# Row maxima of a sliding-window attention: one matmul of 384 columns for three key blocks, half a head group at a time

## Chip, core, metric

The kernel runs on one core of one Trainium2 chip, as one program. The metric is the device time of one execution in microseconds, the median of repeated runs. All computation is fp32; matrix products that need full accuracy are built from "fp32r" halves (a value is split into a high part and a remainder, and three of the four cross products are summed).

## What is computed

A mixer block over 2048 tokens of 512 channels. Attention has 32 heads of 16 channels and looks back over a window of 256 keys; its result is gated by an MLP on the same normalised input.

```python
S, D, H, Dh, W, F = 2048, 512, 32, 16, 256, 1792
xn = layernorm(x)
# attention
q, k, v = split(xn @ wqkv)                      # 32 heads of 16
scores = q @ k.T * Dh ** -0.5
mask = (i - j >= 0) & (i - j < 256)             # i: query, j: key
s = (softmax(where(mask, scores, -1e9)) @ v) @ wo
# gate
g = silu(gelu(layernorm(xn) @ w1 + b1) @ w2 + b2)
return x + s * g
```

## The kernel before, in words

**Stages.** Four layernorm chunks with the first projections (to about 60 us of the span), the attention (60 to 418 us), and the MLP with the output projection (418 us to the end).

**The attention's order is written out by hand.** The 32 heads are eight groups `n` of four heads; a group's four heads are two pairs `p`, and within a pair two heads `a`, one on rows 0 to 63 and one on rows 64 to 127 of the PE array, which run side by side (one such pair of matmuls is called a wave here). The loop over `u` makes 64 units: unit `u` takes key blocks `kb` and `kb + 1` of 128 keys of group `u // 8`. A unit is two steps, `t = 2u` and `t = 2u + 1`. Every call in the loop issues its instructions at once, and each engine runs them in the order in which they were issued (`Ordered` keeps that order for PE, DVE, ACT and POOL; SP, which issues the DMAs, has one queue too). `plan` (`at`) and `ends` (`behind`) hold what is to be issued in the middle and at the end of a given step; `fills` holds matmuls of other work that are laid into the steps: the q/k projections of later groups, the v projections (steps 56 to 73), and the MLP's first layer for the first 512 tokens (from step 98).

**A unit's work.** `prob_part(u, part)` multiplies keys with queries into the two banks of `stb` (8 waves a unit over three parts), ACT takes the exponential into `pt`, POOL zeroes what the mask forbids. `pv_part(u)` multiplies the probabilities with v into `otb`, columns of `zo`; ACT copies that to `oraw` (two buffers), and SP stores it to `oT_d` two steps on.

**The maxima.** The scores are shifted by each query's maximum before the exponential, by an extra row of the query operand. So the maxima of 128 queries (a block `qb`) are computed `LEAD` = 12 steps ahead: in step `t` those of block `m = t + 12`, one block a step. The window of a query block covers three key blocks: its own (lower triangle), the middle one (whole), and the one before that (upper triangle). `max_ends` multiplies with the two ends (one strided matmul of 256 columns for each of the four heads, into the two banks of `xy`); `copy_predicated` then overlays the two triangles with the mask `upper`, and a `tensor_reduce` takes the maximum. `max_middle` multiplies with the middle block (four matmuls of 128 columns into columns 0 to 255 of the two banks of `zo`, named `mids`), with a `tensor_reduce` of its own. `otb` lies in columns 256 to 511 of zo's second bank. Every fourth block `max_rows` takes the minimum of the (negated) two parts, splits it, transposes it and sends it through `mT_d` into the query operand.

**Order in a unit before.** Even step: `prob_part(u, 1)`, ends into xy, middle into zo; on DVE the copy, the reduction of zo, the reduction of xy; then fills. Odd step: `prob_part(u, 2)`, middle into zo with its reduction, two thirds of the fills, ends into xy with copy and reduction, `max_rows` if due, the rest of the fills, `prob_part(u + 1, 0)`, `pv_part(u)`. In the first unit of a group all fills of the odd step come after `prob_part(u + 1, 0)`.

**Other transfers.** `stage_in` copies `w1`, `w2` and `wo` into an order of its own in DRAM (16 steps of 4, from step 23). `keep_xt` stores the normalised input of chunks 1 to 3 (twelve transfers of 512 KB, every fourth step from 25 to 69). `fetch_scales` spreads a row of 512 per-token scales over 128 partitions; before, into a tile of its own at step 80 (`scales_0`) and again, after the attention, into `scales`.

**PSUM.** Eight banks of 512 fp32 columns: `xy`, `zo`, `stb` and `fb` have two each. The program orders any two engines that touch the same bank of one tile, whichever columns they touch.

Of the kernel before, what the change touches and what calls it, by code (L numbers as in the profile page):

```python
# [9 lines left out]
F32 = mybir.dt.float32  # L10
F32R = mybir.dt.float32r
I32 = mybir.dt.int32
# [37 lines left out]
def mixer_kernel(ctx, tc, x, wqk, wv, wo, w1, b1, w2, b2, out):  # L50
# [131 lines left out]
    zo = psum.tile([P, 2, 512], F32, name="zo")  # L182
    otb = zo[:, 1, 256:512]
    mids = zo[:, :, 0:256].rearrange("q a (p k) -> q a p k", p=2)
    ends_of = xy.rearrange("q a (p e k) -> q a p e k", p=2, e=2)
    psf = attn.enter_context(tc.tile_pool(name="psf", bufs=1, space=PSUM))
# [37 lines left out]
    clear_rows(0, ((nc.vector, 0, 1536), (nc.scalar, 4096, 7168), (nc.gpsimd, 1536, 4096), (nc.gpsimd, 7168, 8192)))  # L224
    scales = None
    mask = upper.bitcast(I32).unsqueeze(1).unsqueeze(1).to_broadcast([P, 2, 2, P])
    b1s = const.tile([P, NF], F32, name="b1s")
# [259 lines left out]
    def pair_h(f):  # L487

        def mm(ps, k, r, **flags):
            kt, (a, b) = k // 3, PASSES[k % 3]  # L490
            return nc.tensor.matmul(ps, w1_part(a, f)[r, P * kt: P * (kt + 1)], mlp["yy"][b][kt][r], **flags)

        def finish(ps, t, copy):
            raw = t2.tile([P, 512], F32, tag="t2", name=f"hr_{f}")
            if 5 < f < 12:
                copy(raw, ps)
            else:
                nc.vector.tensor_mul(raw, ps, scales)
            if f < 4:
                soon[f] = raw  # L500
            else:
                behind(t, nc.sync.dma_start, h_d[f - 6], raw)
        return 3 * KT, mm, finish
# [53 lines left out]

    def max_places(n, qb):

        if (n, qb // 4) not in mts:  # L560
            mts[n, qb // 4] = small.tile([P, 2, 2, 2, 4], F32, tag="mt", name=f"mt_{n}_{qb}", bufs=2)
        return (mts[n, qb // 4][:, i, :, :, qb % 4] for i in range(2))

    def max_ends(n, qb):

        mt, _ = max_places(n, qb)
        for p in range(2):
            for a in (1, 0):
                if qb < 2:
                    max_scores(ends_of[:, a, p, 0], n, qb, a, p, lambda row: row[:, P * qb: P * qb + 1].to_broadcast([64, P]))  # L570
                    max_scores(ends_of[:, a, p, 1], n, qb, a, p, lambda row: row[:, P * qb: P * (qb + 1)])
                else:
                    max_scores(ends_of[:, a, p], n, qb, a, p,
                               lambda row: row.rearrange("d (b k) -> d b k", k=P)[:, qb - 2: qb + 1: 2])
        own = ends_of[:, :, :, 1]
        outs["max"] = nc.vector.copy_predicated(own, mask, ends_of[:, :, :, 0]),
        return lambda: nc.vector.tensor_reduce(out=mt, in_=own, axis=AX.X, op=ALU.max, negate=True)

    def max_middle(n, qb):

        if qb == 0:
            return
        _, mu = max_places(n, qb)
        for p in range(2):
            for a in (1, 0):
                max_scores(mids[:, a, p], n, qb, a, p, lambda row: row[:, P * (qb - 1): P * qb])
        nc.vector.tensor_reduce(out=mu, in_=mids, axis=AX.X, op=ALU.max, negate=True)

    def max_block(n, qb):

        rest = max_ends(n, qb)
        max_middle(n, qb)
        rest()

    def max_rows(n, c, t):

        both = mts.pop((n, c))
        mt = both[:, 0]
        mh = small.tile([P, 2, 2, 2, 4], F32R, tag="mh", name=f"mh_{n}_{c}", bufs=2)
        pairs = slice(0 if c else 1, 4)  # L600
        nc.vector.tensor_tensor(mt[:, :, :, pairs], mt[:, :, :, pairs], both[:, 1, :, :, pairs], op=ALU.min)
        eng = nc.gpsimd if t >= -1 else nc.vector
        eng.tensor_copy(mh[:, :, 0], mt)
        eng.tensor_tensor(mh[:, :, 1], mt, mh[:, :, 0].bitcast(F32), op=ALU.subtract)
        mT = small.tile([P, 32], F32, tag="mT", name=f"mT_{n}_{c}", bufs=2)

        for fn, args in todo_dve:
            fn(*args)
        todo_dve.clear()
        nc.vector.transpose(mT, mh.rearrange("p a l i b -> p (a l i b)").bitcast(F32))  # L610
        rows = mT_d[n, c]

        def bring_in():
            nc.sync.dma_start(slots[n % 2][3:P:32, 0, :, 512 * c: 512 * (c + 1)].bitcast(F32),
                              rows.rearrange("(h p b) t -> h p (b t)", h=4, p=2))
        (at if t < 0 else behind)(t + (t < 0), nc.sync.dma_start, rows.rearrange("r (i t) -> i r t", i=4), mT)
        behind(t + 1 + (t < 0), bring_in)
# [46 lines left out]
    def pv_part(u):  # L664

        n, kb = u // 8, 2 * (u % 8)
        seq = [(kb, lambda j: pts[u, j // 2][:, j % 2, 128:384], 0, 256),
               (kb + 1, lambda j: pts[u, j // 2][:, j % 2, 0:128], 128, 256)]
        if kb:
            seq[:0] = [(kb - 1, lambda j: pts[u - 1, 2][:, j % 2, 256 * (j // 2): 256 * (j // 2 + 1)], 0, 256),  # L670
                       (kb - 2, lambda j: pts[u - 1, j // 2][:, j % 2, 384:512], 0, 128)]
        for i, (k, of, lo, hi) in enumerate(seq):
            for j in range(4):
                nc.tensor.matmul(otb[32 * j: 32 * j + DH + 1, lo: hi], vt[:, k, (4 * n + j) % 16], of(j),
                                 start=(i == 0), stop=(i == len(seq) - 1),
                                 skip_group_check=True, tile_position=(0, 32 * j))
        oraw = sgp.tile([P, 256], F32, tag="or", name=f"oraw_{u}", bufs=2)
        nc.scalar.copy(oraw, otb)
        cols = slice(P * kb, P * (kb + 2))
        at(2 * u + 2, nc.sync.dma_start, oT_d[n, :, :, cols].rearrange("j r t -> (j r) t"), oraw)  # L680
# [4 lines left out]
    def scale_parts():  # L685
# [20 lines left out]
        def power(c):  # L706
            at = sv[:, 4 * c: 4 * c + 4]
            nc.gpsimd.tensor_tensor(at, at, mhalf, op=ALU.pow)
        return variance, ratio, power

    def fetch_scales(c, dst):
# [165 lines left out]
    for b in range(4):  # L877
        behind(73 + b, nc.sync.dma_start, s_d[:, b], svT[32 * b: 32 * b + 4 * NCH])
    def open_scales():
        nonlocal scales  # L880
        scales = bigp.tile([P, 512], F32, tag="wa", name="scales_0")
        fetch_scales(0, scales)
    behind(80, open_scales)
    for k in range(KT * (NCH - 1)):
        behind(25 + 4 * k, keep_xt, 1 + k // KT, k % KT)
    by_vector = nc.vector.tensor_copy
# [8 lines left out]
    for f, t, lo_at, lo_by in ((6, 90, 93, nc.vector), (7, 95, 96, nc.vector), (8, 96, 98, on_pool), (9, 99, 101, nc.vector),  # L895
# [5 lines left out]
        at(lo_at, settle, "w1", f, None, lo_by)  # L901
    at(113, open_w2, 0)
    for f in range(W2_FIRST):
        at(114 + f // 2, fetch, "w2", f)
        at(121 + f, settle, "w2", f, by_vector, nc.vector)
# [10 lines left out]

    def first_h(f, scaled=True):

        for k in range(3 * KT):
            hidden_mm(fb[f], f, k)  # L920
        ready[f] = t2.tile([P, 512], F32, tag="t2", name=f"hf_{f}")
        if scaled:
            nc.vector.tensor_mul(ready[f], fb[f], scales)
        else:
            nc.vector.tensor_copy(ready[f], fb[f])

# [31 lines left out]

    def own_max(part, m):
        return part(m // 16, m % 16) if m < end else lambda: None  # L960

# [26 lines left out]
    for u in range(end // 2):  # L988
        t = 2 * u
        prob_part(u, 1)  # L990
        rest = own_max(max_ends, t + LEAD)
        own_max(max_middle, t + LEAD)
        rest()
        calm[0] = t < end - LEAD
# [5 lines left out]
        prob_part(u, 2)  # L1000
        own_max(max_middle, t + LEAD)
        todo = fills.get((t, 0), [])
        n = sum(fn.__name__ == "unit" for fn, _ in todo)
        now[:] = t, 0
        run(delayed.pop((t, 0), ()))
        n -= n if u % 8 == 0 else n // 3
        for fn, args in todo[:n]:
            fn(*args)
        planned(t)
        fill_in(t, 1)  # L1010
        own_max(max_ends, t + LEAD)()
        calm[0] = False
# [19 lines left out]
    nc.sync.on = False  # L1032
    first_h(1, False)

# [11 lines left out]
    scales = cp.tile([P, 512], F32, name="scales")  # L1046
    fetch_scales(0, scales)
    wos = cp.tile([P, 2, 4, 512], F32R, name="wos")
# [8 lines left out]

    nc.gpsimd.tensor_tensor(ready[1], ready[1], scales, op=ALU.mult)
    for f in range(6, NF, 2):
# [3 lines left out]
        for k in range(2 if f < 12 else 0):  # L1063
            nc.gpsimd.tensor_tensor(t[:, k], t[:, k], scales, op=ALU.mult)
        if f == 8:
            den = fetch_sums()
    nc.sync.dma_start(b2s, bass.AP(tensor=b2.tensor, offset=b2.offset, ap=[[0, P], [1, 512]]))

# [443 lines left out]
```

## Time and profile before

| what | value |
|---|---|
| median of 3 runs | 737.12 us (735.98 to 738.46) |
| the profiled execution | 737.41 us |
| its span, first to last instruction | 735.7 us |
| mean granted clock | 0.998 |
| busy: PE, DVE, ACT, POOL | 717.6, 507.7, 411.7, 298.9 us |

The profile shows one execution. Its views used here: the page (busy time by engine, groups of instructions with count, busy time and mean duration), the windows (busy time by stretch), the timeline (instructions in order of time, like ones merged: start, length, engine, operation, `out<-in`, count, idle time before and what ended it), the waits (who waited for whom: total us, times, longest) and the chain of waits (the work that ended last, followed back). "PEld" is the weight load ahead of a matmul. All instructions are recorded under the line of one helper (L42), so groups are told apart by their tiles: `xy<-qk` and `zo<-qk` are matmuls of the maxima, `zo<-pt,vt` the output (each fp32 matmul is recorded twice), `stb<-qk` the scores, `fb<-xnT,wqb` fills, `mt<-` the reductions.

### The profile page before, as it was taken

How to read it: one execution, taken by the hardware profiler on the slowest of the kernel's cores; microseconds unless marked ns; L12 is line 12 of the kernel's file. 1: busy time of each engine (PE TensorE's matmuls, PEld its weight loads, DVE VectorE, ACT ScalarE, POOL GpSimd, SP SyncE). 2: the span in 40 equal slices, each digit the busy share in tenths (PEclk: the TensorE clock that was granted, in tenths of full speed). 3: DMA queues.
4: the chain of work that ended last, by engine and by line, in shares of the span. 5: the costliest groups of instructions: out<-in, count | busy, mean ns of one | idle time of the engine just before them, and what ended most of it. 6: DMA issues, size and time to landing. Idle time of an engine off the chain costs nothing.

```text
span 735.7 us, 17763 instructions
## 1 busy us (share of the span) xinstructions
PE 717.6 (98%) x6944; PEld 580.7 (79%) x6944; DVE 507.7 (69%) x863; ACT 411.7 (56%) x628; POOL 298.9 (41%) x500
## 2 busy tenths in 40 slices
PE   8999999998899999999999999999999999999997
PEld 7998777776678887777777787888888888888886
DVE  7886787876677667778884667536687855667823
ACT  7767777766577566777877726232353734541001
POOL 7344666755468554676777550113202000001102
PEclk9999999999999999999999999999999999999999
DMA  8325455767787733667824465547213322163701
GB/s 294 79 48 126 96 137 142 201 179 205 200 236 202 207 113 97 160 157 192 222 75 153 154 219 147 195 130 238 91 58 104 104 79 86 63 186 113 253 16 58
DMA packets 66275, 106.95 MB, mean 145 GB/s; under 512 B 12624, under 2 KB 21072, under 8 KB 66192
## 3 DMA queue, kind: packets, MB, share of 16 engines
q1 hardware_dynamic: 66192, 105.82, 50.5%
q8 instruction: 55, 0.90, 0.5%
q14 instruction: 28, 0.23, 0.1%
HBM read 54.80 MB, written 33.82 MB: 120 GB/s over the span
## 4 chain that ended last, share of the span: by engine, by line
PE 90%; ACT 3%; DMA 3%; DVE 2%; issue 1%; SPq 0%; POOL 0%; ACTq 0%; DVEq 0%
PE acc L42 20%; PE fb L42 19%; PE zo L42 15%; PE p L42 9%; PE stb L42 7%; PE s L42 6%; PE h L42 6%; PE xy L42 5%; ACT pt L42 2%; PE pv L42 2%; DMA oT_d<-oraw 2%; DMA qk<-sh 1%; DVE mt L42 1%; DMA x<-in_x_dram 1%; SPq L42 0%
## 5 line engine op out<-in xcount | busy, mean ns | idle before, releaser
L42 ACT ACTIVATE pt<-stb 128x1024 f32<-128x1024 f32 (+1 forms) x176 | 177.7, 1009 | 51.7 <-PE stb L42 47.4
L42 POOL TENSOR_SCALAR_AFFINE_SELECT pt<-pt 128x512 f32<-128x512 f32 (+1 forms) x296 | 162.7, 569 | 86.7 <-ACT pt L42 85.8
L42 DVE COPY_PREDICATED xy<-upper,xy 128x512 f32<-128x512 int32 x128 | 88.9, 695 | 61.8 <-PE xy L42 61.6
L42 POOL TENSOR_TENSOR xo<-xo,gated 128x512 f32<-128x512 f32 x15 | 19.9, 1329 | 220.1 <-DVE gated L42 219.1
L42 PE MATMUL fb<-xnT,wqb 64*128 64x512 f32 (+2 forms) x732 | 105.9, 393 | 0.2 <-DVE xy L42 0.2
L42 PE MATMUL acc<-w,gh 128*128 128x512 f32 x320 | 98.7, 390 | 1.5 <-ACT gh L42 1.5
L42 PE MATMUL zo<-pt,vt 128*17 128x128 f32 (+1 forms) x1920 | 90.5, 327 | 0.0
L42 DVE TENSOR_REDUCE mt<-xy 128x4 f32<-128x512 f32 x128 | 88.0, 688 | 2.3
L42 DVE TENSOR_REDUCE mt<-zo 128x4 f32<-128x512 f32 x120 | 82.7, 689 | 6.9 <-PE zo L42 6.4
L42 PE MATMUL stb<-qk 64*128 64x384 f32 (+1 forms) x704 | 76.7, 296 | 2.1 <-ACT pt L42 2.1
L42 PEld LDWEIGHTS stb<-qk 64*128 64x128 f32 x704 | 58.9, 186 | 23.1 <-ACT pt L42 9.4
L42 PEld LDWEIGHTS zo<-pt,vt 128*17 128x17 f32 x1920 | 48.9, 97 | 33.3 <-issue 1.8
L42 PEld LDWEIGHTS acc<-w,gh 128*128 128x128 f32 x320 | 60.0, 188 | 14.3 <-ACT gh L42 1.9
L42 PEld LDWEIGHTS fb<-xnT,wqb 64*128 64x128 f32 (+1 forms) x732 | 61.8, 188 | 6.4 <-DVE xy L42 0.4
L42 PE MATMUL xy<-qk 64*128 64x256 f32 (+2 forms) x608 | 62.2, 291 | 1.1 <-DVE mt L42 1.1
L42 PE MATMUL acc<-w,gl 128*128 128x512 f32 x160 | 62.5, 391 | 0.0
L42 PEld LDWEIGHTS xy<-qk 64*128 64x128 f32 x608 | 48.6, 187 | 8.3 <-DVE mt L42 2.3
L42 PE MATMUL zo<-qk 64*128 64x128 f32 x480 | 48.8, 281 | 6.1 <-ACT oraw L42 5.4
L42 PE MATMUL p<-xnT 128*128 128x512 f32 x189 | 51.8, 389 | 0.0
L42 PEld LDWEIGHTS zo<-qk 64*128 64x128 f32 x480 | 36.3, 186 | 16.0 <-ACT oraw L42 6.9
L42 PE MATMUL s<-wos,ohl 128*128 128x512 f32 (+1 forms) x204 | 44.3, 377 | 0.0
L42 ACT ACTIVATE gated<-acc 128x512 f32<-128x512 f32 x16 | 8.7, 595 | 61.9 <-DVE acc L42 61.9
(210 smaller groups left out, 1212.4 us busy)
## 6 DMA issues: line engine op xcount, KB each, us to landing
qk<-sh SPq DMA_DIRECT2D x128, 128.0 KB
qk<-pjr SPq DMA_DIRECT2D x64, 128.0 KB
oT_d<-oraw SPq DMA_DIRECT2D x64, 128.0 KB
w_d<-in_w_dram SPq DMA_DIRECT2D x14, 512.0 KB
xt_d<-xnT SPq DMA_DIRECT2D x12, 512.0 KB
x<-in_x_dram SPq DMA_DIRECT2D x16, 256.0 KB
w<-w_d SPq DMA_DIRECT2D x16, 256.0 KB
or<-oT_d SPq DMA_DIRECT2D x16, 256.0 KB
```

Of the source, the lines that this page charges most:

```text
L42: r = issue(*args, **kwargs)
```

## The change

The maxima of one pair `p` (half of a block's four heads) become `max_part(n, qb, p)`: for each of the two heads one matmul of 384 columns over all three key blocks (blocks 0 and 1 of a group have fewer), pair 0 in the two banks of `xy`, pair 1 in the two banks of `zo`, columns 0 to 383. The function returns the DVE work: a `copy_predicated` of 256 elements that overlays the triangles, and one `tensor_reduce` of 512 over own and middle block. `max_rows` has no minimum to take any more. `otb` becomes columns 384 to 511 of both banks of zo, one bank for each of the unit's two query blocks; `pv_part` issues 24 matmuls of 128 columns instead of 16 of 256 and 128.

Order in a unit after: even step: pair 0's matmuls into xy, `prob_part(u, 1)`, pair 1's into zo, DVE's work for xy, then for zo, then fills. Odd step: `prob_part(u, 2)`, a quarter of the fills, pair 1 into zo with its DVE work, the other fills (in a group's first unit up to half of them), pair 0 into xy with its DVE work, `max_rows`, `prob_part(u + 1, 0)`, the remaining fills, `pv_part(u)`.

The first scales go into a free corner of w2's tile (`first_scales`), fetched at step 114; `first_h(1)` multiplies by them directly; the fetch into `scales` comes after that of the sums. `keep_xt` moves to every second step from 56 to 78.

```diff
-    otb = zo[:, 1, 256:512]
-    mids = zo[:, :, 0:256].rearrange("q a (p k) -> q a p k", p=2)
-    ends_of = xy.rearrange("q a (p e k) -> q a p e k", p=2, e=2)
+    otb = zo[:, :, 384:512]
...
-    scales = None
-    mask = upper.bitcast(I32).unsqueeze(1).unsqueeze(1).to_broadcast([P, 2, 2, P])
+    mask = upper.bitcast(I32).unsqueeze(1).to_broadcast([P, 2, P])
...
-                nc.vector.tensor_mul(raw, ps, scales)
+                nc.vector.tensor_mul(raw, ps, first_scales())
...
-    def max_places(n, qb):
+    def max_part(n, qb, p):
         if (n, qb // 4) not in mts:
-            mts[n, qb // 4] = small.tile([P, 2, 2, 2, 4], F32, tag="mt", name=f"mt_{n}_{qb}", bufs=2)
-        return (mts[n, qb // 4][:, i, :, :, qb % 4] for i in range(2))
-    def max_ends(n, qb):
...
-    def max_middle(n, qb):
...
+            mts[n, qb // 4] = small.tile([P, 2, 2, 4], F32, tag="mt", name=f"mt_{n}_{qb}", bufs=2)
+        mt, bank = mts[n, qb // 4], zo if p else xy
+        if qb < 2:
             for a in (1, 0):
+                max_scores(bank[:, a, 0:P], n, qb, a, p, lambda row: row[:, P * qb: P * qb + 1].to_broadcast([64, P]))
+        for a in (1, 0):
+            max_scores(bank[:, a, 384 - P * min(3, qb + 1): 384], n, qb, a, p,
+                       lambda row: row[:, P * max(0, qb - 2): P * (qb + 1)])
+
+        def maximum():
+            own = bank[:, :, 256:384]
+            outs["max"] = nc.vector.copy_predicated(own, mask, bank[:, :, 0:P]),
+            nc.vector.tensor_reduce(out=mt[:, :, p, qb % 4], in_=bank[:, :, 128:384] if qb else own, axis=AX.X,
+                                    op=ALU.max, negate=True)
+        return maximum
...
     def max_rows(n, c, t):
-        both = mts.pop((n, c))
-        mt = both[:, 0]
+        mt = mts.pop((n, c))
...
-        nc.vector.tensor_tensor(mt[:, :, :, pairs], mt[:, :, :, pairs], both[:, 1, :, :, pairs], op=ALU.min)
...
     def pv_part(u):
-        seq = [(kb, lambda j: pts[u, j // 2][:, j % 2, 128:384], 0, 256),
-               (kb + 1, lambda j: pts[u, j // 2][:, j % 2, 0:128], 128, 256)]
+        seq = [(0, kb, lambda j: pts[u, j // 2][:, j % 2, 128:256]), (1, kb, lambda j: pts[u, j // 2][:, j % 2, 256:384]),
+               (1, kb + 1, lambda j: pts[u, j // 2][:, j % 2, 0:128])]
...
-                nc.tensor.matmul(otb[32 * j: 32 * j + DH + 1, lo: hi], vt[:, k, (4 * n + j) % 16], of(j),
+                nc.tensor.matmul(otb[32 * j: 32 * j + DH + 1, h], vt[:, k, (4 * n + j) % 16], of(j),
...
+    def first_scales():
+        return mlp["w2", 0][:, 7168:7680].bitcast(F32)
...
-    behind(80, open_scales)
     for k in range(KT * (NCH - 1)):
-        behind(25 + 4 * k, keep_xt, 1 + k // KT, k % KT)
+        behind(56 + 2 * k, keep_xt, 1 + k // KT, k % KT)
...
     at(113, open_w2, 0)
+    at(114, lambda: fetch_scales(0, first_scales()))
...
         t = 2 * u
+        one = own_max(t + LEAD, 0)
         prob_part(u, 1)
-        rest = own_max(max_ends, t + LEAD)
-        own_max(max_middle, t + LEAD)
-        rest()
+        two = own_max(t + LEAD, 1)
+        one()
+        two()
...
         prob_part(u, 2)
-        own_max(max_middle, t + LEAD)
...
-        n -= n if u % 8 == 0 else n // 3
-        for fn, args in todo[:n]:
+        first, n = n // 4, n // 2 if u % 8 == 0 else n
+        for fn, args in todo[:first]:
+            fn(*args)
+        own_max(t + LEAD, 1)()
+        for fn, args in todo[first:n]:
             fn(*args)
         planned(t)
         fill_in(t, 1)
-        own_max(max_ends, t + LEAD)()
+        own_max(t + LEAD, 0)()
...
-    first_h(1, False)
+    first_h(1)
...
-    fetch_scales(0, scales)
...
-    nc.gpsimd.tensor_tensor(ready[1], ready[1], scales, op=ALU.mult)
...
         if f == 8:
             den = fetch_sums()
+            fetch_scales(0, scales)
```

More of the change, by code (lines that the diff above doesn't have):

```diff
@@ L556, in max_scores @@
         nc.tensor.matmul(out, slot[r, 0, p, P * qb: P * (qb + 1)], keys(slot[r, 1, p]), start=True, stop=True)
-    def max_places(n, qb):
+    def max_part(n, qb, p):
         if (n, qb // 4) not in mts:
-            mts[n, qb // 4] = small.tile([P, 2, 2, 2, 4], F32, tag="mt", name=f"mt_{n}_{qb}", bufs=2)
-        return (mts[n, qb // 4][:, i, :, :, qb % 4] for i in range(2))
-    def max_ends(n, qb):
-        mt, _ = max_places(n, qb)
-        for p in range(2):
-            for a in (1, 0):
[L569 to L577, printed above, removed]
@@ L579, in max_middle @@
-    def max_middle(n, qb):
[L581 to L587, printed above, removed]
+            mts[n, qb // 4] = small.tile([P, 2, 2, 4], F32, tag="mt", name=f"mt_{n}_{qb}", bufs=2)
+        mt, bank = mts[n, qb // 4], zo if p else xy
@@ L589, in max_block @@
+        return maximum
     def max_block(n, qb):
-        rest = max_ends(n, qb)
-        max_middle(n, qb)
-        rest()
+        rest = [max_part(n, qb, p) for p in range(2)]
+        for part in rest[::-1]:
+            part()
     def max_rows(n, c, t):
-        both = mts.pop((n, c))
-        mt = both[:, 0]
+        mt = mts.pop((n, c))
         mh = small.tile([P, 2, 2, 2, 4], F32R, tag="mh", name=f"mh_{n}_{c}", bufs=2)
-        pairs = slice(0 if c else 1, 4)
-        nc.vector.tensor_tensor(mt[:, :, :, pairs], mt[:, :, :, pairs], both[:, 1, :, :, pairs], op=ALU.min)
@@ L666, in pv_part, with last @@
         n, kb = u // 8, 2 * (u % 8)
-        seq = [(kb, lambda j: pts[u, j // 2][:, j % 2, 128:384], 0, 256),
-               (kb + 1, lambda j: pts[u, j // 2][:, j % 2, 0:128], 128, 256)]
+        seq = [(0, kb, lambda j: pts[u, j // 2][:, j % 2, 128:256]), (1, kb, lambda j: pts[u, j // 2][:, j % 2, 256:384]),
+               (1, kb + 1, lambda j: pts[u, j // 2][:, j % 2, 0:128])]
         if kb:
-            seq[:0] = [(kb - 1, lambda j: pts[u - 1, 2][:, j % 2, 256 * (j // 2): 256 * (j // 2 + 1)], 0, 256),
-                       (kb - 2, lambda j: pts[u - 1, j // 2][:, j % 2, 384:512], 0, 128)]
-        for i, (k, of, lo, hi) in enumerate(seq):
+            def last(j, h):
+                return pts[u - 1, 2][:, j % 2, 256 * (j // 2) + 128 * h: 256 * (j // 2) + 128 * (h + 1)]
+            seq[:0] = [(0, kb - 2, lambda j: pts[u - 1, j // 2][:, j % 2, 384:512]), (0, kb - 1, lambda j: last(j, 0)),
+                       (1, kb - 1, lambda j: last(j, 1))]
+        halves = [i for i, *_ in seq]
+        for i, (h, k, of) in enumerate(seq):
             for j in range(4):
-                nc.tensor.matmul(otb[32 * j: 32 * j + DH + 1, lo: hi], vt[:, k, (4 * n + j) % 16], of(j),
-                                 start=(i == 0), stop=(i == len(seq) - 1),
+                nc.tensor.matmul(otb[32 * j: 32 * j + DH + 1, h], vt[:, k, (4 * n + j) % 16], of(j),
+                                 start=(h not in halves[:i]), stop=(h not in halves[i + 1:]),
                                  skip_group_check=True, tile_position=(0, 32 * j))
         oraw = sgp.tile([P, 256], F32, tag="or", name=f"oraw_{u}", bufs=2)
-        nc.scalar.copy(oraw, otb)
+        nc.scalar.copy(oraw.rearrange("j (h t) -> j h t", h=2), otb)
         cols = slice(P * kb, P * (kb + 2))
@@ L878, in mixer_kernel @@
         behind(73 + b, nc.sync.dma_start, s_d[:, b], svT[32 * b: 32 * b + 4 * NCH])
-    def open_scales():
-        nonlocal scales
-        scales = bigp.tile([P, 512], F32, tag="wa", name="scales_0")
-        fetch_scales(0, scales)
-    behind(80, open_scales)
     for k in range(KT * (NCH - 1)):
-        behind(25 + 4 * k, keep_xt, 1 + k // KT, k % KT)
+        behind(56 + 2 * k, keep_xt, 1 + k // KT, k % KT)
     by_vector = nc.vector.tensor_copy
@@ L915, in activate_first, with first_h @@
             ready[f] = t[:, 2 * k], t[:, 2 * k + 1]
-    def first_h(f, scaled=True):
+    def first_h(f):
         for k in range(3 * KT):
@@ L921, in first_h @@
         ready[f] = t2.tile([P, 512], F32, tag="t2", name=f"hf_{f}")
[L922 to L925, printed above, removed]
+        nc.vector.tensor_mul(ready[f], fb[f], first_scales())
     ready = {}
@@ L957, in mixer_kernel, with own_max @@
     end = 16 * NQ
-    def own_max(part, m):
-        return part(m // 16, m % 16) if m < end else lambda: None
+    def own_max(m, p):
+        return max_part(m // 16, m % 16, p) if m < end else lambda: None
     def own_rows(m, t):
@@ L989, in mixer_kernel @@
         t = 2 * u
+        one = own_max(t + LEAD, 0)
         prob_part(u, 1)
-        rest = own_max(max_ends, t + LEAD)
-        own_max(max_middle, t + LEAD)
-        rest()
+        two = own_max(t + LEAD, 1)
+        one()
+        two()
         calm[0] = t < end - LEAD
@@ L1046, in mixer_kernel @@
     scales = cp.tile([P, 512], F32, name="scales")
-    fetch_scales(0, scales)
     wos = cp.tile([P, 2, 4, 512], F32R, name="wos")
@@ L1063, in mixer_kernel @@
         for k in range(2 if f < 12 else 0):
-            nc.gpsimd.tensor_tensor(t[:, k], t[:, k], scales, op=ALU.mult)
+            nc.gpsimd.tensor_tensor(t[:, k], t[:, k], first_scales(), op=ALU.mult)
         if f == 8:
             den = fetch_sums()
+            fetch_scales(0, scales)
     nc.sync.dma_start(b2s, bass.AP(tensor=b2.tensor, offset=b2.offset, ap=[[0, P], [1, 512]]))
```

## The prediction

> **What bounds the kernel now.** I read the page first, then the windows by stage.
>
> ```profile
> span 735.7 us, 17763 instructions
> PE 717.6 (98%) x6944; PEld 580.7 (79%) x6944; DVE 507.7 (69%) x863; ACT 411.7 (56%) x628; POOL 298.9 (41%) x500
> 166.00:206.00 40.00, 34.32 (x452) 25.71 (x444) 26.41 (x44) 23.99 (x35) 20.81 (x37) 0.96 0.78 208
> 245.00:278.00 33.00, 32.33 (x550) 27.94 (x544) 21.08 (x37) 21.46 (x32) 18.32 (x35) 1.00 0.49 139
> 278.00:392.00 114.00, 112.60 (x1542) 85.12 (x1540) 91.17 (x153) 85.60 (x124) 75.22 (x131) 1.00 0.59 155
> ```
>
> In a window the columns after the length are busy time of PE, PEld, DVE, ACT and POOL, the granted clock and the DMA share. PE is nearly always busy, but from 278 to 392 us DVE has 91.17 of 114 us: little room. Between 166 and 206 PE stood idle for 5.7 us. The chain of waits gives the length of a unit (two steps, one `pv_part`), from one group of 32 output records to another:
>
> ```profile
> 160.40 1.43 PE zo L42 x32
> 172.03 3.94 DMA oT_d<-oraw
> 199.83 1.43 PE zo L42 x32
> 257.17 1.42 PE zo L42 x32
> 276.19 1.42 PE zo L42 x32
> 292.33 1.43 PE zo L42 x32
> 303.53 1.43 PE zo L42 x32
> 336.11 1.43 PE zo L42 x32
> ```
>
> An ordinary unit, with 16 fill matmuls of 512 columns, takes 5.43 us (six from 303.53 to 336.11). The six from 160.40 take 39.43 us, so 6.85 us is stall, with stores of `oraw` as links. In the stage of the v projections a unit takes 6.34 us (three from 257.17). The timeline shows one unit:
>
> ```profile
> 315.69 0.50 PE L42 MATMUL stb<-qk 64*128 64x384 f32 x4
> 316.03 0.45 PE L42 MATMUL xy<-qk 64*128 64x256 f32 x4
> 316.32 0.38 PE L42 MATMUL zo<-qk 64*128 64x128 f32 x4
> 316.52 0.69 DVE L42 COPY_PREDICATED xy<-upper,xy 128x512 f32<-128x512 int32 x1 [0.17 <-PE xy L42]
> 316.53 1.15 PE L42 MATMUL fb<-xnT,wqb 64*128 64x512 f32 x8
> 317.16 0.69 DVE L42 TENSOR_REDUCE mt<-zo 128x4 f32<-128x512 f32 x1
> 317.51 0.40 PE L42 MATMUL stb<-qk 64*128 64x256 f32 x4
> 317.77 0.68 DVE L42 TENSOR_REDUCE mt<-xy 128x4 f32<-128x512 f32 x1
> 317.91 0.44 PE L42 MATMUL zo<-qk 64*128 64x128 f32 x4
> 318.18 0.92 PE L42 MATMUL fb<-xnT,wqb 64*128 64x512 f32 x6
> 318.94 0.40 PE L42 MATMUL xy<-qk 64*128 64x256 f32 x4
> 319.19 0.40 PE L42 MATMUL fb<-xnT,wqb 64*128 64x512 f32 x2
> 319.39 0.70 DVE L42 COPY_PREDICATED xy<-upper,xy 128x512 f32<-128x512 int32 x1 [0.31 <-PE xy L42]
> 319.42 0.40 PE L42 MATMUL stb<-qk 64*128 64x384 f32 x4
> 319.75 1.50 PE L42 MATMUL zo<-pt,vt 128*17 128x256 f32 x32
> 320.12 0.69 DVE L42 TENSOR_REDUCE mt<-xy 128x4 f32<-128x512 f32 x1
> 321.17 0.44 PE L42 MATMUL stb<-qk 64*128 64x384 f32 x2
> ```
>
> Starts are what counts; durations of matmuls overlap. The middle matmuls at 317.91 start just where the reduction of zo ended (317.16 + 0.69 + 0.06): the hand-over PE to DVE to PE is already as tight as PE. The waits say the same, and something else:
>
> ```profile
> PEld zo L42 <- ACT oraw L42: 6.9, 8, 2.0
> PEld zo L42 <- DVE mt L42: 5.3, 18, 0.6
> ```
>
> The middle matmuls write columns 0 to 255 of zo, `oraw` is read from 256 to 511 of its second bank, and yet they wait for that copy. Sharing a bank orders two engines even where their columns differ.
>
> **The change, part by part.** *Maximum matmuls on PE.* A block's eight matmuls (four of 256 columns, four of 128) become four of 384; per unit, xy and zo take 0.29 + 0.21 + 0.27 + 0.25 = 1.02 us by the starts above. Two matmuls in the two row halves run side by side, a wave: 0.12 us for 256 columns (0.25 for two), 0.245 for 512 (0.98 for four). So 384 columns take 0.18, and four waves 0.72, of which one stands first in the unit and costs 0.1 more. Gain on PE: some 0.2 to 0.45 us a unit, taken as 0.4 with the lead-in of short waves.
>
> *Output on PE.* Sixteen matmuls in eight waves become 24 in twelve over the same 768 columns, which took 1.42 us (319.75 to 321.17). Four more waves cost nothing if columns alone count, 0.2 us if each costs half a wave of 128. I take 0.02, the nearer to how 512 and 256 columns scale: 1.44 us.
>
> So PE alone would need about 5.05 us a unit. DVE decides against it.
>
> *Maxima on DVE.*
>
> ```profile
> L42 DVE COPY_PREDICATED xy<-upper,xy 128x512 f32<-128x512 int32 x128 | 88.9, 695 | 61.8 <-PE xy L42 61.6
> L42 DVE COPY vt<-fb 128x256 f32<-128x256 f32 x1 | 0.4, 425 | 1.1 <-PE fb L42 1.1
> L42 PE MATMUL stb<-qk 64*128 64x384 f32 x214 | 42.8, 396 | 2.1 <-ACT pt L42 2.1
> ```
>
> Each half now needs its own predicated copy of 256 elements and its own reduction of 512. No predicated copy of 256 is in the trace; it lies between 0.35 us (half of 0.695) and 0.695. A plain copy of 256 out of PSUM took 0.425, so I take 0.43. The reduction keeps 0.69. A block costs 2.24 us instead of 2.07. The minimum over two parts, once in four blocks, goes from DVE's queue; it stood off the path, so nothing is counted for it.
>
> *The new round trip.* Before, zo was free after one copy and one reduction. Now in the even step xy is served first and zo second, and the odd step's first maximum matmuls need zo. Let T be the unit's first matmul. Its wave lasts 0.44 (321.17), DVE follows 0.05 later (318.94 + 0.40 to 319.39): copy at T+0.49, reduction 0.46 later (0.43 + 0.03; 319.39 to 320.12 is 0.73 = 0.70 + 0.03), next copy 0.61 after it (317.16 to 317.77), second reduction 0.46 after that, end 0.69 later: T+2.71. PE may write zo at T+2.77. It arrives sooner: 0.28 + 0.24 (scores) + 0.18 + 0.98 + 0.25 (scores) + 0.25 (the first quarter of the fills) = T+2.2. It waits 0.55 us, and behind it in PE's queue stand the other fills, the xy maxima, the next scores and the output.
>
> *The second wait.* The output columns now lie in both banks of zo, so `pv_part` cannot write until the odd step's zo reduction has ended: matmul 0.40 + 0.05, copy 0.46, reduction 0.69, hand-over 0.06 = 1.66 us after zo was written. PE's own work between is 0.18 + 0.74 + 0.18 + 0.33 = 1.43: another 0.23 us of waiting, with the next unit behind it. Before, zo's last maximum matmuls (317.91) came 1.84 us ahead of the output (319.75), and one reduction of 0.69 fitted between.
>
> Together a unit takes 2.77 + 1.66 + 1.44 = 5.87 us, against 5.43: +0.44. With the copy at its bounds (three lie on this path) 5.63 to 6.67. What is late next: ACT, whose copy of `oraw` holds the even zo matmuls, has room inside the 2.7 us.
>
> Here a rule bears on the change. The Trainium skill, "PSUM — Partial Sum Buffer", section "PSUM bank collisions raise a hardware error", asks that engines be kept apart by bank and quadrant, not by address. The trace agrees: the 6.9 us waits above are between different columns. By address alone the second wait would vanish and the unit be 5.64 us (below); that is the first rival below.
>
> *How many units.* Of the 64, 39 take the whole round trip: 39 x 0.44 = +17.2 us. The 6 whose maxima are those of a group's blocks 0 and 1 reduce 256 elements instead of 512 in the even step, 0.52 less, and come out near 5.4: 0. The 6 that begin a group have half the output work: the same sum with 0.79 for 1.44 gives 5.2, before 5.77 (292.33 to 303.53 less 5.43); I count half of the 3.4, -1.8, since their other waits are not all seen. The first unit is left at 0, and the last six have no maxima.
>
> *v stage.* There PE has 24 waves of 256 for fills, and the round trip is covered: 2.77 + (0.18 + 1.08 + 0.18 + 0.33) + 1.44 = 5.98 instead of 6.34; six units, -2.2. Twelve blocks ahead of the attention, where PE always has other work: four waves of 0.12 against two of 0.18 save 0.12 each, -1.4.
>
> *`keep_xt` moved from steps 25 to 69 to steps 56 to 78.*
>
> ```profile
> xt_d<-xnT SPq DMA_DIRECT2D x12, 512.0 KB
> 164.01 0.60 SPq L42 DMA_DIRECT2D xt_d<-xnT  x1
> SPq L42 <- DMA mT_d<-mT: 10.3, 4, 2.9
> ```
>
> Eight of twelve transfers leave the steps where the stall of 6.85 us is, each with 0.60 us of SP's queue, where row maxima, q/k rows and `oraw` stores stand behind it; SP itself waited 10.3 us between 130 and 206 us for slow landings. They join the v stage, DMA share 0.49, past the staging copies. Gain between 0 and 6.85; loss in the new place between 0 and the same. I take -5.5: the stall lies where the queue was fullest, and longer units relieve it too.
>
> *Scales.*
>
> ```profile
> 428.95 1.29 POOL L42 TENSOR_TENSOR hf<-hf,scales 128x512 f32<-128x512 f32 x1 [12.96 <-DMA scales<-s_d]
> PE acc L42 <- ACT gh L42: 1.5, 1, 1.5
> ```
>
> Fetched at step 114 into the corner of `w2`, used at 121; seven steps cover a landing. At the change of stage the product that POOL began after a wait of 12.96 us becomes one on DVE in place of a copy of the same tile, and the second fetch moves behind that of the sums on SP's queue. After the attention PE waits once, 1.5 us, for another tile; so 0. If the cover went, the first scaled tile would be late by the fetch, up to 4 us.
>
> **The sum.** 17.2 - 1.8 - 2.2 - 1.4 - 5.5 = +6.3 us. The profiled execution took 737.41 us (span 735.7), by 0.29 above the median of 737.12, so 744 us.
>
> **Rivals.** *Faster, no second wait:* the output does not wait for the zo reduction. Unit 2.77 + 1.43 + 1.44 = 5.64, +0.21; 39 x 0.21 less the 10.9 of the other terms = -2.7: 735 us, and 732 with copies of 0.40 (two on the path). Against it, the `oraw` waits. *Faster, PE-bound:* DVE's halves hide behind PE, a unit is 5.1 us; 39 x -0.33 - 6 x 0.3 - 10.9 = -25.6: 712 us. For it, DVE's work is only about 4.9 us a unit; against it, both round trips. It decides once zo comes free within 2.2 us of the unit's start. *No relief from the moved transfers:* +5.5, 749 us. *A draw:* copies of 0.38 (unit 5.72) and all of the stall gone: 39 x 0.29 - 5.4 - 6.85 = -0.9, 736.5 us.
>
> **How the numbers follow.** Forecast 0.50 (its own range 739 to 751), no relief 0.12, draw 0.13, no second wait 0.12, PE-bound 0.13. A difference under 0.3% (2.2 us) cannot be told from none. Slower: 0.62; same: 0.13; faster: 0.25. The range leaves out the PE-bound end and the longest copies: 729 to 752.
>
> **What would show it.** Right: ordinary units of 5.8 to 5.9 us in the chain; PE waits on DVE's mt before zo matmuls of 0.5 us, some 40 times, and of 0.2 before the output; DVE busy 19 us more; no 6.85 us stall at 166 to 206. Wrong: units of 5.1 to 5.6 us, output starting inside a reduction of zo, predicated copies well off 0.43 us, or stalls moved to 230 to 290.

## The result, and the profile after

The changed kernel takes 749.44 us (749.37 to 749.86, four runs); the kernel before took 737.75 us beside it (735.98 to 738.46, four runs). The ratio is 1.0163, with a 95% interval of 1.0143 to 1.0184: slower by 11.7 us. The forecast was 744.0. The profiled execution took 749.37 us.

The head of the page after, with the engines' shares of the chain of waits:

```profile
span 747.4 us, 18911 instructions
PE 719.3 (96%) x7424; PEld 582.0 (78%) x7424; DVE 527.3 (71%) x967; ACT 414.6 (55%) x628; POOL 298.7 (40%) x499
PE 72%; DVE 15%; issue 4%; ACT 4%; POOL 3%; DMA 1%; SPq 1%; ACTq 0%; POOLq 0%
```

Before, the same line of the chain read:

```profile
PE 90%; ACT 3%; DMA 3%; DVE 2%; issue 1%; SPq 0%; POOL 0%; ACTq 0%; DVEq 0%
```

PE's busy time is nearly what it was (717.6), while the span has grown by 11.7 us: the new time is idle time of PE, and DVE, 2% of the chain before, is 15% of it now. DVE's busy time rose by 19.6 us. Its groups, shapes kept apart:

```profile
L42 DVE TENSOR_REDUCE mt<-zo 128x2 f32<-128x512 f32 x120 | 83.2, 693 | 4.1
L42 DVE COPY_PREDICATED zo<-upper,zo 128x256 f32<-128x256 int32 x128 | 54.3, 425 | 41.0 <-PE zo L42 40.9
L42 DVE COPY_PREDICATED xy<-upper,xy 128x256 f32<-128x256 int32 x128 | 54.1, 422 | 20.4 <-PE xy L42 18.0
```

One predicated copy of 512 elements (695 ns) became two of 256 at 425 and 422 ns: 108.4 us together instead of 88.9. The waits of the whole span name the place:

```profile
PEld zo L42 <- DVE mt L42: 34.6, 82, 1.0
PE zo L42 <- DVE mt L42: 10.6, 49, 0.6
```

PE's weight loads for zo waited 5.3 us, 18 times, for a reduction before; now 34.6 us, 82 times, about two for each unit of the full round trip. The timeline shows the two in one unit:

```profile
318.08 0.44 PE L42 MATMUL xy<-qk 64*128 64x384 f32 x2
318.36 0.40 PE L42 MATMUL stb<-qk 64*128 64x384 f32 x4
318.57 0.43 DVE L42 COPY_PREDICATED xy<-upper,xy 128x256 f32<-128x256 int32 x1 [0.91 <-PE xy L42]
318.69 0.45 PE L42 MATMUL zo<-qk 64*128 64x384 f32 x2
318.98 1.09 PE L42 MATMUL fb<-xnT,wqb 64*128 64x512 f32 x8
319.03 0.69 DVE L42 TENSOR_REDUCE mt<-xy 128x2 f32<-128x512 f32 x1
319.64 0.42 DVE L42 COPY_PREDICATED zo<-upper,zo 128x256 f32<-128x256 int32 x1
319.94 0.50 PE L42 MATMUL stb<-qk 64*128 64x256 f32 x4
320.09 0.69 DVE L42 TENSOR_REDUCE mt<-zo 128x2 f32<-128x512 f32 x1
320.29 0.39 PE L42 MATMUL fb<-xnT,wqb 64*128 64x512 f32 x2
320.84 0.44 PE L42 MATMUL zo<-qk 64*128 64x384 f32 x2 [0.17 <-DVE mt L42]
321.32 0.43 DVE L42 COPY_PREDICATED zo<-upper,zo 128x256 f32<-128x256 int32 x1 [0.54 <-PE zo L42]
321.79 0.69 DVE L42 TENSOR_REDUCE mt<-zo 128x2 f32<-128x512 f32 x1
321.98 0.40 PE L42 MATMUL stb<-qk 64*128 64x384 f32 x4
322.53 1.50 PE L42 MATMUL zo<-pt,vt 128*17 128x128 f32 x48 [0.16 <-DVE mt L42]
323.97 0.45 PE L42 MATMUL xy<-qk 64*128 64x384 f32 x2
```

Read it from one reduction of zo to the matmul behind it. The even one ends at 320.09 + 0.69 = 320.78, and the odd step's maxima go into zo at 320.84. The odd one ends at 322.48, and the output starts at 322.53. PE had been ready for both some 0.2 to 0.3 us sooner: the two fills at 320.29 take 0.245, and the scores at 321.98 take 0.33. In the chain, two outputs, three units apart:

```profile
328.42 1.50 PE zo L42 x48
346.08 1.50 PE zo L42 x48
```

A unit takes (346.08 - 328.42) / 3 = 5.89 us, 5.43 before.

### The profile page after: what moved, and what is told of

Its sections match the earlier page's. It is cut to its first block, busy times and chain, and to the rows that moved or that the text cites. A ratio compares the mean times of both kernels' runs of the same rounds, so it can differ in the third digit from the quotient of the medians.

```text
span 747.4 us, 18911 instructions
## 1 busy us (share of the span) xinstructions
PE 719.3 (96%) x7424; PEld 582.0 (78%) x7424; DVE 527.3 (71%) x967; ACT 414.6 (55%) x628; POOL 298.7 (40%) x499
## 4 chain that ended last, share of the span: by engine, by line
PE 72%; DVE 15%; issue 4%; ACT 4%; POOL 3%; DMA 1%; SPq 1%; ACTq 0%; POOLq 0%
PE acc L42 20%; PE zo L42 14%; PE fb L42 9%; PE p L42 9%; DVE mt L42 8%; PE s L42 6%; PE h L42 6%; DVE zo L42 4%; PE xy L42 4%; PE stb L42 2%; DVE xy L42 2%; ACT pt L42 2%; POOL pt L42 1%; PE pv L42 1%; ACT sh L42 1%
## 5 line engine op out<-in xcount | busy, mean ns | idle before, releaser
L42 PE MATMUL zo<-pt,vt 128*17 128x128 f32 x2880 | 91.1, 274 | 6.7 <-DVE mt L42 3.3
L42 DVE TENSOR_REDUCE mt<-zo 128x2 f32<-128x512 f32 (+1 forms) x128 | 86.6, 676 | 4.4
L42 DVE TENSOR_REDUCE mt<-xy 128x2 f32<-128x512 f32 (+1 forms) x128 | 86.6, 676 | 4.4
L42 PEld LDWEIGHTS zo<-pt,vt 128*17 128x17 f32 x2880 | 73.3, 97 | 19.8 <-DVE mt L42 15.4
L42 DVE COPY_PREDICATED zo<-upper,zo 128x256 f32<-128x256 int32 x128 | 54.3, 425 | 41.0 <-PE zo L42 40.9
L42 DVE COPY_PREDICATED xy<-upper,xy 128x256 f32<-128x256 int32 x128 | 54.1, 422 | 20.4 <-PE xy L42 18.0
L42 PE MATMUL zo<-qk 64*128 64x384 f32 (+2 forms) x288 | 54.1, 390 | 8.3 <-DVE mt L42 7.3
L42 PE MATMUL xy<-qk 64*128 64x384 f32 (+2 forms) x320 | 53.8, 357 | 1.1 <-DVE mt L42 0.4
L42 PEld LDWEIGHTS zo<-qk 64*128 64x128 f32 x288 | 26.1, 184 | 27.9 <-DVE mt L42 19.2
L42 PEld LDWEIGHTS xy<-qk 64*128 64x128 f32 x320 | 28.9, 184 | 18.4 <-issue 11.1
```

The costliest lines, as they stand in the source:

```text
L42: r = issue(*args, **kwargs)
```

## Experiments

**Is it the round trip through zo?** The rivals were PE's work and DVE's total of work. Three kernels shorten one kind of reduction each: zo in the even step, zo in the odd step and, as a control, xy in the odd step, which no wait seemed to stand on. All three take the same 0.5 us from DVE's total in each unit.

```diff
-    def max_part(n, qb, p):
+    def max_part(n, qb, p, short=False):
...
-  in_=bank[:, :, 128:384] if qb else own
+  in_=bank[:, :, 256:272] if short else bank[:, :, 128:384] if qb else own
...
-        two = own_max(t + LEAD, 1)              # even step, zo: first kernel
+        two = own_max(t + LEAD, 1, True)
...
-        own_max(t + LEAD, 1)()                  # odd step, zo: second kernel
+        own_max(t + LEAD, 1, True)()
...
-        own_max(t + LEAD, 0)()                  # odd step, xy: third kernel
+        own_max(t + LEAD, 0, True)()
```

> The changed kernel, but the even step's reduction of zo reads 32 of its 512 elements, so it leaves out part of those maxima. Round trip (my theory: a unit is set by xy and zo being served one after the other before zo comes free, then by the output waiting for zo): the reduction takes about 0.19 instead of 0.69 us and lies on the path; PE then reaches the odd step's zo matmuls at about the unit's start + 2.35, so a unit goes from 5.89 to 5.4-5.5 us and the kernel from 749.4 to 731-734. DVE's total work sets the unit (rival): 0.5 us less in each of about 57 units, 721-727, and the same for any of DVE's reductions. PE's own work sets it (24 output matmuls and their weight loads; rival): no change, 749.

> The changed kernel, but the odd step's reduction of zo reads 32 of its 512 elements, so it leaves out part of those maxima. Round trip: it shortens the second wait only (output waiting for zo), and PE's own work between takes 1.43 of the 1.66 us, so a unit falls by some 0.2-0.25 us: 739-742. DVE's total work: the same gain as with the even step's reduction, 721-727. PE's own work: 749.

> The changed kernel, but the odd step's reduction of xy reads 32 of its 512 elements, so it leaves out part of those maxima. Round trip: this reduction is off the path (xy is free 0.4 us before it is written again): 747-750, the control of the other two. DVE's total work: 721-727 as with any other reduction. PE's own work: 749.

Measured, one execution each, against 749.44: 735.06 (-14.4), 738.48 (-11.0) and 747.45 (-2.0); the kernel before took 738.56 beside them. The first gained 1 us less than the round trip had been expected to give, the second half a us more. The same work taken from DVE is worth 14.4 us in one place, 11.0 in the next and 2.0 in the third, so its total does not set the unit, nor do PE's matmuls, which are the same in all three. The waits of the first kernel, then of the second:

```profile
PE zo L42 <- DVE mt L42: 1.5, 9, 0.2
PEld zo L42 <- DVE mt L42: 13.5, 49, 0.5
```

```profile
PE zo L42 <- DVE mt L42: 7.0, 29, 0.6
PEld zo L42 <- DVE mt L42: 18.8, 37, 1.0
```

Each takes away about one of the two waits in a unit (82 became 49 and 37) and leaves the other.

The control is not wholly off the path. Of its 2.0 us, 1.4 lie in the seven units behind a group's first one: a group's first unit has half the output work, so PE comes back to xy before the odd step's reduction has left it. One such place in the changed kernel, where that reduction ends at 306.55:

```profile
305.86 0.69 DVE L42 TENSOR_REDUCE mt<-xy 128x2 f32<-128x512 f32 x1
306.60 0.19 PEld L42 LDWEIGHTS xy<-qk 64*128 64x128 f32 x2 [0.40 <-DVE mt L42]
```

With the shorter reduction these seven units take 5.95 us on average instead of 6.15; the ordinary ones hardly change (5.89 for 5.91).

**Order alone.** In the odd step the two halves change places: pair 0 into xy early, pair 1 into zo late, ahead of the scores and the output. The work of every engine stays.

```diff
-        own_max(t + LEAD, 1)()
+        own_max(t + LEAD, 0)()
         for fn, args in todo[first:n]:
             fn(*args)
         planned(t)
         fill_in(t, 1)
-        own_max(t + LEAD, 0)()
+        own_max(t + LEAD, 1)()
```

> The changed kernel, but in the odd step pair 0 (xy) comes early and pair 1 (zo) late, nothing else moved. Round trip: zo is written at about the unit's start + 3.3 instead of 2.77, DVE serves it after xy and the output can start at about + 5.05 instead of + 4.4: a unit of about 6.5 us, 770-776. DVE's total work or PE's own work, which are the same in both orders: 748-751.

Measured: 791.07 us, 41.6 above the changed kernel. Its timeline, around one output:

```profile
340.09 0.34 PE L42 MATMUL zo<-qk 64*128 64x384 f32 x2
341.12 0.69 DVE L42 TENSOR_REDUCE mt<-zo 128x2 f32<-128x512 f32 x1
341.87 1.39 PE L42 MATMUL zo<-pt,vt 128*17 128x128 f32 x44 [1.20 <-DVE mt L42]
```

The output comes 1.78 us after zo was written, as in the other kernels about 1.7 (1.69 above), but now only 0.6 us of PE's work lies between, and PE idles 1.20 us. The direction and the place were expected; the size was set too low by 15 us or more. The expected unit of 6.5 us was right for the ordinary ones, which average 6.57; the rest, counted at nothing, is in the others, which grew too: 0.9 us in each of the six of the v stage, 1.1 in each of the five with short reductions, 0.8 in each of the six that begin a group.

**Can the first wait be traded away?** In the even step DVE serves zo first.

```diff
-        one()
         two()
+        one()
```

> The changed kernel; in the even step DVE serves zo before xy, with the same work. Round trip by hand, from the unit's first matmul T: zo is written at T+0.61, its copy starts at T+1.10 (0.5 later than that of xy did), its reduction ends at T+2.25, so the first wait falls from 0.55 to under 0.1. But xy comes after it (copy T+2.17, reduction T+2.63) and the odd step's zo copy starts only at T+3.24 and its reduction ends at T+4.39; PE would be there at T+3.74: the second wait grows from 0.2 to 0.7. Unit 4.45 + 1.44 = 5.89, as before: 746 to 752. If the first wait alone were the cost, it goes for 38 units: about 730 to 733. If DVE's total of work bounds the unit, no change either, but then with no longer wait at the output.

Measured: 749.80 us, no change. One unit, from its first matmul at 318.20:

```profile
318.81 0.44 PE L42 MATMUL zo<-qk 64*128 64x384 f32 x2
319.83 0.69 DVE L42 TENSOR_REDUCE mt<-zo 128x2 f32<-128x512 f32 x1
320.63 0.39 PE L42 MATMUL zo<-qk 64*128 64x384 f32 x2
320.89 0.69 DVE L42 TENSOR_REDUCE mt<-xy 128x2 f32<-128x512 f32 x1
321.95 0.69 DVE L42 TENSOR_REDUCE mt<-zo 128x2 f32<-128x512 f32 x1
322.70 1.50 PE L42 MATMUL zo<-pt,vt 128*17 128x128 f32 x48 [0.39 <-DVE mt L42]
```

The odd step's zo matmuls at 320.63 no longer wait. But xy's reduction now stands ahead of zo's in DVE's queue, the odd one ends only at 322.64, and the output's wait has grown from 0.16 to 0.39 us. The output started 4.50 us into the unit, against 4.45 by hand. The wait of 0.30 us that was removed came back almost whole behind it.

**Both waits gone: what comes next?** The first two edits together.

> The changed kernel; the reductions of zo in the even and in the odd step read 32 of their 512 elements each (leaves out part of those maxima). Round trip with two waits: the gains of the two alone add up (14.4 and 11.0), 749.4 - 25.4 = 724, and an ordinary unit of about 5.88 - 0.31 - 0.21 = 5.36. If PE's own work is the 5.05 us of the prediction and nothing else binds, the gains more than add up, unit 5.05 to 5.2, 716 to 721. If a third limit stands close behind (ACT's exponential, the two banks of xy), the gains overlap: 728 to 733.

Measured, one execution: 730.51 us, not the 724 of the two gains added: 18.9 of 25.4. The reductions hardly hold PE any more:

```profile
PEld zo L42 <- DVE mt L42: 2.2, 5, 0.5
PE zo L42 <- ACT oraw L42: 3.3, 4, 1.9
PE stb L42 <- ACT pt L42: 1.8, 6, 0.4
```

So the time of the third outcome came about, but ACT's exponential, the limit that it names first, explains little of it: PE itself waited 1.8 us for `pt` in all. Another 2 us are one unit of 7.41 us (at 358 to 366 us of the span), in which PE waited 1.9 us for a copy into `oraw`, and that copy waited for a store. A unit in its timeline, at the same place as above:

```profile
320.24 0.44 PE L42 MATMUL xy<-qk 64*128 64x384 f32 x2
324.16 1.50 PE L42 MATMUL zo<-pt,vt 128*17 128x128 f32 x48
325.59 0.44 PE L42 MATMUL xy<-qk 64*128 64x384 f32 x2
```

It takes 325.59 - 320.24 = 5.35 us, where the prediction's sum of PE's work was 5.05. The unit of the changed kernel agrees with the 5.35: without its two waits, 0.30 and 0.22 us, its 5.89 us are 5.37. Most of the 0.3 is in three groups there that the sum priced by their columns alone: the scores at 318.36 took 0.33 us (0.24 in the sum), zo's maxima at 318.69 took 0.29 (0.18) and the scores at 319.94 took 0.35 (0.25). Ahead of the first two no weight load waits; ahead of the third one had waited 0.31 us for ACT, so a part of that 0.1 may be ACT's. So the next limit is mostly PE's own work, which the sum had too short. The 27 ordinary units outside the stall and the v stage average 5.48 us here (5.41 without the long one), 5.43 in the kernel before: on PE itself the change shows next to no saving, where the prediction had counted about 0.4 us a unit.

**Is it the split of the output?** The kernel before, with its output as 24 matmuls of 128 columns where it was.

```diff
-        seq = [(kb, lambda j: pts[u, j // 2][:, j % 2, 128:384], 0, 256),
-               (kb + 1, lambda j: pts[u, j // 2][:, j % 2, 0:128], 128, 256)]
+        seq = [(kb, lambda j: pts[u, j // 2][:, j % 2, 128:256], 0, 128),
+               (kb, lambda j: pts[u, j // 2][:, j % 2, 256:384], 128, 256),
+               (kb + 1, lambda j: pts[u, j // 2][:, j % 2, 0:128], 128, 256)]
```

> The kernel before with only the output changed to 24 matmuls of 128 columns (12 waves) in the 256 columns that it had. By the prediction's term (columns alone count, 0.02 us a unit) +1 us for some 51 full units: 738 to 740. If each of the four more waves costs half a wave of 128 (0.2 us a unit): +8 to +10, 746 to 748, and then a third of the 11.7 us of the change would be this split.

Measured: 739.15 us against 737.53 beside it, ratio 1.0013 (0.9991 to 1.0035). Its units in the timeline:

```profile
318.70 1.50 PE L42 MATMUL zo<-pt,vt 128*17 128x128 f32 x48
324.17 1.50 PE L42 MATMUL zo<-pt,vt 128*17 128x128 f32 x48
329.61 1.50 PE L42 MATMUL zo<-pt,vt 128*17 128x128 f32 x48
```

5.46 us each, against 5.43 (over the 27 ordinary units 5.44 against 5.43): the four more waves cost a few hundredths, and the interval leaves room for 2.6 us at most. The split into more waves is not the cause; that the output now lies in both banks of zo is the second wait above.

**What is the rest of the change worth?** The transfers moved alone, in the kernel before; then that with the scales in w2's corner and all that goes with it; and the changed kernel with the transfers put back.

```diff
-        behind(25 + 4 * k, keep_xt, 1 + k // KT, k % KT)
+        behind(56 + 2 * k, keep_xt, 1 + k // KT, k % KT)
```

> The kernel before with one part of the change alone: keep_xt in steps 56 to 78. If the queue of SP and its transfers made the stall of 6.85 us at 166 to 206 us, the six units there go from 6.57 to about 5.45 us and the kernel from 737.7 to 731-732.5. If the transfers only move their stall to the later steps: 736-739.

> The kernel before with all of the change but the maxima and the output: keep_xt late, scales in the corner of w2, one product on DVE at the change of stage, the second fetch of scales behind the sums. The changed kernel was 2.3 us shorter from the last unit with maxima to the end; if the scales did that, this kernel is 2 us below the one with keep_xt alone, 729-730.5. If it came from something else: equal to that one.

> The changed kernel with keep_xt back in steps 25 to 69. If the moved transfers are worth their whole 6.85 us here too: 756. If the longer units (0.45 us of waiting each) had absorbed the stall anyway: 749.5-751. I expect 750-753.

Measured: 731.49 us, ratio to the kernel before 0.9933 (0.9906 to 0.9960); 731.34 us, 0.9914 (0.9882 to 0.9946); and 749.95 us, 1.0175 (1.0145 to 1.0206). So the two edits that have nothing to do with the maxima gain some 6 us, and **the kernel before with both of them beats both kernels**; between it and the moved transfers alone the intervals do not decide. The maxima and the output alone cost about 18 us (749.4 less 731.3). The median of the second is not the 2 us below the first that had been expected; the last stage, below, shows that gain, and a longer stall in its profiled execution hides it (36.7 us for the six units of the stall, 34.6 in that of the first). In the changed kernel, putting the transfers back costs 0.5 us by the medians, and the runs overlap (749.77 to 750.68 against 749.37 to 749.86). PE's waits between 155 and 206 us show where the difference lies. First the kernel before, then with the transfers moved alone, then the changed kernel with the transfers put back:

```profile
PE zo L42 <- ACT oraw L42: 5.4, 4, 1.8
```

```profile
PE zo L42 <- ACT oraw L42: 1.8, 3, 1.0
```

```profile
PE zo L42 <- ACT oraw L42: 0.4, 1, 0.4
```

The move relieves the stall in part, in a profiled execution of 733.28 us, 1.8 above its median. The new maxima and output relieve it nearly wholly, with no move at all. The likely reason is the longer unit, which gives a store 5.9 us instead of 5.4 to land; no run changes that alone.

The scales edit shows in the last stage. From the attention's last output in the chain to the end of the span it is 735.7 - 416.27 = 319.4 us before and 747.4 - 430.15 = 317.2 after; 731.6 - 412.01 = 319.6 with the transfers alone and 731.8 - 414.49 = 317.3 with the scales too.

**The start.** Ahead of the attention, PE waits at a change of PSUM rows for the operation kept as `outs["max"]`. Before, that was the one copy of a block; after, every call sets it, and the last stands. Here only the copy on zo sets it.

```diff
-            outs["max"] = nc.vector.copy_predicated(own, mask, bank[:, :, 0:P]),
+            made = nc.vector.copy_predicated(own, mask, bank[:, :, 0:P])
+            if p:
+                outs["max"] = made,
```

> The changed kernel, but the point that PE waits for when projection banks change rows (the last predicated copy issued, ahead of the attention) is always the copy on zo, which DVE serves first there, as it was DVE's first instruction of a block in the kernel before. The changed kernel starts the attention 1.7 us late, where I had counted a gain of 1.4; it shows three waits of about 0.9-1.1 us of PE for that copy. If they are it: 746-747.5. If they only cover other waits: 749.

Measured: 748.11 us (748.00 to 748.17), 1.3 less, between the two outcomes expected. In the changed kernel PE's waits between 18 and 72 us are:

```profile
PE fb L42 <- POOL sv L42: 1.3, 1, 1.3
PE fb L42 <- DVE xy L42: 1.1, 2, 0.9
PE pair_-3_949 L42 <- DVE xy L42: 0.9, 1, 0.9
```

With this edit the two on `DVE xy` are gone and the one on POOL stays. Where that one comes from was not tried.

## Why the prediction was right, and where its sizes were off

The direction and the mechanism were the predicted ones; the size was little more than half of what came (6.3 of 11.7 us). Zo came free for the odd step 2.76 us after the unit's first matmul (318.08 to 320.84; predicted 2.77), the output followed 1.69 us later (1.66), and lasted 1.44 (1.44): 5.89 us against 5.87. One term of the unit was off: PE came to the first wait 2.46 us into the unit (320.54) and not 2.2, because its work up to there had been priced too low, so that it waited 0.30 and not 0.55. That this left the length of the unit alone is luck: zo came free later still, and the wait swallowed the error.

The second wait, which the first rival denied, is there: the output waits for reductions of other columns of its banks, and shortening those gave 11.0 us. The prediction cites for it the Trainium skill, "PSUM — Partial Sum Buffer", section "PSUM bank collisions raise a hardware error", which says to keep engines apart by bank and quadrant and not by address. The waits agree with that in so far as this program itself orders engines by bank; what the chip would do if two engines did meet in one bank, no run here shows.

The PE-bound rival fell by the waits. Its unit of 5.1 us was out of reach in any case, since PE takes 5.37 without its two waits: with both waits nearly gone the kernel stands at 730.5 us and not at 712.

The spans differ by 11.7 us, the sum was 6.3. Periods between the last output waves of the units, taken from the two profiles and added up by class, give:

| where | predicted, us | measured, us |
|---|---|---|
| to the end of the first output | -1.4 | +1.7 |
| 27 ordinary units outside the stall (0.44 each) | +11.9 | +13.0 |
| 7 units behind a group's first one | +3.1 | +5.1 |
| 5 units with 256-element reductions (outside the stall) | 0 | +1.3 |
| 6 that begin a group | -1.8 | -1.9 |
| 6 of the stall (5 x 0.44, less 5.5) | -3.3 | -4.2 |
| 6 of the v stage | -2.2 | -1.0 |
| the last six, and the stage after | 0 | -2.3 |

The step that was mis-sized most is the start, by 3.1 us: the prediction counted the saved waves and not that `outs["max"]` names a later operation now. That is 1.3 us by the run; 1.3 us of waiting for POOL stands beside it. The next is a class that had been counted as ordinary. The seven units behind a group's first one take 6.15 us instead of 5.87: they have a third wait, for the odd step's reduction of xy, and shortening that gave 0.20 us of each. The units with short reductions were taken as free and cost 0.27 each; what holds them was not tried. The v stage gained half of its 2.2. On the other side the scales edit, taken as 0, gained 2.2 at the change of stage, where PE's wait of 1.5 us for ACT's `gh` is gone.

The stall went as the sum had it, -4.2 for -3.3, but for a reason that the prediction gave half a sentence ("longer units relieve it too"). The reason it put first, the moved transfers, gains 6.7 us by the medians in the kernel with short units and 0.5 in the changed one. The rival "no relief", at 749 us, names the measured time by chance: the relief came, and other terms made up for it.

## What to carry to other kernels

Before merging operations to save work on the busiest engine, write down for each buffer who holds it and for how long, round the whole loop; here PE's own work hardly fell (some 5.37 us a unit, 5.43 before) and its waits grew, because zo then served two copies, two reductions and an output in both banks in each unit. Price the work that is to be saved from rows of short groups, not by columns alone. A wait that was removed by reordering came back here at the next user of the same buffer; only work taken out of the round trip shortened the unit. Test the unrelated edits of a change by themselves: two of them gained 6 us, and the main one cost 18.

## What had not been expected

The kernel before varies more than the one after: 734.43 to 739.99 us over 14 runs, against 749.37 to 749.86 over four. The stall that moves is the one at units 18 to 23, 39.4 us in the profile before and 42.6 in that with the split output, of which nothing is left in the slower kernel (35.2 us, 5.87 a unit). The clock has a part in it that the prediction did not count: from 194 to 202 us of the profile before, the granted clock was 0.79 and a fill matmul of 512 columns took 566 ns on average, against 406 ns from 186 to 194 us at 1.00. With the split output the clock was 0.50 and 0.68 in the two stretches of 4 us from 198 to 206 us, and one output took 2.05 us instead of 1.50. From 166 to 206 us it was 1.00 with the transfers moved alone and in the changed kernel. What lowered it was not tried. A reduction of 32 elements out of PSUM took 0.19 us, one of 512 took 0.69, and a predicated copy of 256 took 0.42 against 0.695 for 512: halving a copy saves 39% of it, so that splitting it in two costs 22% more.
